# A gated recurrence and an MLP on one core: both MLP products regrouped from blocks of 256 and 192 columns to 38 products of blocks of 128

## The chip, the cores and the metric

The program runs on one core of a Trainium2 chip. TensorE (PE, with its weight loads as PEld) multiplies matrices into PSUM; VectorE (DVE), ScalarE (ACT) and GpSimd (POOL) work elementwise, POOL on SBUF alone; SyncE (SP) issues nearly all DMA transfers. Each engine takes its instructions in the order in which they were recorded and waits where data or a buffer is not ready. The metric is the device time of one execution in microseconds.

## The reference

A recurrence over 768 tokens, for 4 batches with 8 heads of 48 channels, and on its output a layer norm and an MLP with a residual:

```python
# q, k, v, alpha: (4, 8, 768, 48), float32
for t in range(S):
    state = alpha[:, :, t, :, None] * state + np.einsum('bhd,bhe->bhde', k[:, :, t], v[:, :, t])
    y[:, :, t] = np.einsum('bhd,bhde->bhe', q[:, :, t], state)
# x = y as (4, 768, 384)
mu = np.mean(x, axis=-1, keepdims=True)
var = np.mean((x - mu) ** 2, axis=-1, keepdims=True)
xn = (x - mu) / np.sqrt(var + 1e-06) * g_ln
ch = np.maximum(xn @ w_ch1, 0.0) @ w_ch2      # 384 -> 1536 -> 384, weights in float64
return (x + ch).astype(np.float32)
```

## The kernel before, in words

**Tiling.** The 768 tokens are 6 chunks of 128. Attention (`attention(c, b)`, L278) handles one chunk of one batch: 24 pieces of work, in which the recurrence becomes products of 64 or 128 tokens, and which ends with the normed tokens transposed into `xT` (3 blocks of 128 channels by 4 batches by 128 tokens). The MLP handles one chunk of all four batches at a time: `x` is 3 by 4 blocks of 128x128, `w1` 3 by 12, `w2` 12 by 3.

**The weights** arrive in float64 in 12 pieces of 768 KB through three staging buffers. `round_weights` (L207) makes float32 of a piece with five VectorE instructions of 768 columns and one of ScalarE.

**The MLP's products.** Chunk 0 uses the plain form: `hidden` (L499), 72 matmuls of 256 columns, and `project` (L514), 48 matmuls of 384 columns. Chunks 1 to 5 use schemes in the manner of Strassen, which trade products for sums of blocks: the first product is 15 products in place of 18 (`hidden_product`, L777; each 2 matmuls of 256 columns, done twice over), the second 20 in place of 24 (`product`, L611; each 4 matmuls of 192 columns). Sums of w1 (`combine_first`), of w2 (`combine_weights`), of x (`combine_x`) and of h (`combine_hidden`) are made on VectorE. Every product goes to a PSUM bank of its own; VectorE adds it to one or more results (L805 to L838, L628, L631), ScalarE copies some, and POOL makes late sums of intermediate results (L814 to L834, L634). ScalarE applies the relu (L846).

**The order of the work** is written out by hand in `ORDER` (L25), a string in which each letter lets one piece of work record its next few instructions, up to its next `yield` (L878): small letters are the 24 pieces of attention, A to L the weight pieces, Y and Z chunk 0's first product, P and Q its second, M the products of chunks 1 to 5, V the first product of the last chunk, S and W the weight sums, X and N the sums of x and h, R the relus, O the loads of the residual. Nothing reorders it: an instruction of an engine stands behind all that were recorded for this engine earlier.

**Buffers.** All PSUM tiles share 8 banks (tag `bank`). `hT` holds the hidden layer of a chunk; the last chunk's lies in buffers of attention that are free by then (`buffers_of_last`). Attention's results wait in DRAM (`kept`) and come back as the residual (`ob`).

Of the kernel before, what the change touches and what calls it, by code (L numbers as in the profile page):

```python
# [9 lines left out]
FP32 = mybir.dt.float32  # L10
# [13 lines left out]

ORDER = (  # L25
    "acacababcdaacabdbaabdcacabbacbbababceccbaAcfcdbadaacecacfeafdedebdfbeadbaedeecge"
    "adbAacgAfedghbgeedfecfafgfcefdAgeddbbgfdfghffbebaigcjbibffhjBhcdcYhCfcgccehYfedh"
    "cfedeedhgdedYjAfidBfjiBZhjhZZfBYegfhgjhghCiZYBYiCYYhfhghhkggZilihjZjgiZCiDjYDZZZ"
    "ghZYEYjkeiYkiDiEijgljjjlghYCYhiYkhYFEZhiFigYEZigkikDYZZlkkeejlYlgjhFlZlmYkZgknlg"
    "jZSGkHmiknlSljlkiljkjlGiHlmlllZimFhmZYgYmmjZiYhmheeHmGlkfSnZlnZefSQnmfiGHZghkkeo"  # L30
    "IYmSkiISkJgjIjommmOmJPJnSnQgopPghlKPIKhKjiPOnLSnSfSXkmQLffQOLXWkimXPQSWmPPXpnOpW"
    "XmnnXSmXSQomWnnpnmSoXmQMlmlkXkWliMnnMoXXpjWSWSMjMMoMoMlSMnMMWMoMknMMpMMqMMMMMOPi"
    "npnMopMMrmOMjkpMpopopRqoMoirQkplppnqprRppqWMMWMMnMWMqlMRrMMMMkMqRMMMjkrqRMrMMpsk"
    "oMoMMqMMRRnqpMMRjMqMMoWqOqsnRpqlsoqqpMsNtRNpMMNMjNoMoMMMosRqMMMOkNooMqtNMNMMMtMo"
    "MRlNNsmkNMpqMMNtMMMNlMrMMNMMNqMtqMsrMMWNnrrqMMMNMMstnMXvMsMMvXXprXorrXXXrqMMMXXM"
    "MMMMMMMsXqMMOmvMMMMMMMuXMMMMMMmtRMmttMRrtMrMMttrstvMtqussvsqtMMMMqMrMMrvMMMrRMMM"
    "MRMtMnMRMMmssmrMrrpOtsORMuRMoRMsMMMMoRNMMNtMMNMpqMMMoRNMRNMNNMMNRNOMnNMMMrstMpMN"
    "toNMNMMMMMrMnuoOMsMuNMvxMMuMNrpMOMNovMMvMMvMpMMMXtXMxvvMsXvssXXsXtvMXMuMXuXMMMMM"
    "usMMMtwMMMMMMvMMvwuuuRuuXuuuLxvXOMMMMMMMMMMMwMwxMrMuMswMuMMMwMMsvRxRvMMsMMRwMMxM"
    "xMqwMxMMxMwRtMMMxwMMMMxRqruwtxRwxswxxwRxwuxwRMNvNwMRMNrvwNRMMMMMMtNwNNquNNRrsvst"  # L40
    "tMNMJxMOMMMNNMxMMMvMqMuwxxMNtMtMMMMxuwXMwMMNXMXMMNMvNMXXuMXMXMMxXMXwMMXwMMMvMwMM"
    "MxMMMMMMMXMMMMMOuMuMMRMMMMMMMMwMMMMMMMMMRMMvxMMRMRxwMMMROMuMRMvOwxMMRRMwMRxMNMOM"
    "uMvMMXRVNMMMXXMMRMXXXXMMNVNVXVVXMVNMMVVVMVRVNXVVVVVNRVVMNXVVMVRVMVMVNVNMNVVVMVMV"
    "VMRVRVMVVVMVMVONVMVMNMVMMMRVMNNVRVVVVMVVROVMMMVMNVRVVRVMVMVMNMVRKMOMMMRNNMNMMNMM"
    "MMMNVNMNMNVMMMMNRONMMMNMMNMMMNMMMMNMMMNMMMMMMM"
# [4 lines left out]
def kernel(  # L50
# [41 lines left out]
    P = 128  # L92
# [89 lines left out]
    w1 = cpool.tile([P, NJ // 2, NF, 2 * P], FP32, name="w1")  # L182
# [9 lines left out]
    for i in range(NJ // 2):  # L192
        cs, js = slice(2 * i * P, 2 * (i + 1) * P), slice(2 * i, 2 * (i + 1))
        pieces.append((w1[:, i], w1_src[:, :, cs]))
        pieces.append((w2[:, js], w2_src[:, js]))
# [43 lines left out]
    more = cpool.tile([P, 4, NJ // 3 * DM // 2], FP32, name="more")  # L239
    zero = more.rearrange("p i m -> p (i m)")[:, 20 * P:21 * P]  # L240
    nc.vector.memset(zero, 0.0)
# [9 lines left out]
    eqs = [cpool.tile([P, NP, 2, 64], FP32, name=f"eq{b}") for b in range(2)]  # L251
    eqs += [shared[:, i * NP * P:(i + 1) * NP * P].rearrange(
        "p (a b c) -> p a b c", b=2, c=64) for i in range(2)]
    qks = [cpool.tile([P, 2, NP, 2, 64], FP32, name=f"qk{b}") for b in range(3)]
# [15 lines left out]
    ats = [cpool.tile([P, NP, 2, 2, HS], FP32, name=f"at{i}") for i in range(2)]  # L270
# [3 lines left out]
    x_of, xT_of, hT_of, las = ({} for _ in range(4))  # L274
# [3 lines left out]
    def attention(c, b):  # L278
# [52 lines left out]
        kT = work.tile([R, NP, 2, HS], FP32, name="kT", tag="sum", bufs=11)  # L331
        qT = work.tile([R, NP, 2, HS], FP32, name="qT", tag="sum", bufs=11)
# [60 lines left out]
        mid = None if whole else work.tile([R, NP, D], FP32, name="mid", tag="mid", bufs=3)  # L393
# [105 lines left out]
    def hidden(h, j):  # L499

        if 0 not in hT_of:
            hT_of[0] = work.tile([P, NJ, B, P], FP32, name="hT", tag="hT", bufs=1)
        bs = slice(2 * h, 2 * h + 2)
        hps = ps.tile([P, 2, P], FP32, name="hps", tag="bank", bufs=8)
        for f in range(NF):
            nc.tensor.matmul(hps, w1[:, j // 2, f, j % 2 * P:][:, :P], xT_of[0][:, f, bs],  # L506
                             start=(f == 0), stop=(f == NF - 1))
        yield
        nc.scalar.activation(out=hT_of[0][:, j, bs], in_=hps, func=AFT.Relu)
        yield  # L510

    ops_of, ob_of = {}, {}

    def project(c, b, js):  # L514
        if js[0] == 0:
            ops_of[b] = ps.tile([P, DM], FP32, name="ops", tag="bank", bufs=8)
        for j in js:
            nc.tensor.matmul(ops_of[b], hT_of[c][:, j, b], w2[:, j],  # L518
                             start=(j == 0), stop=(j == NJ - 1))
        yield  # L520
        if js[-1] == NJ - 1:
            nc.vector.tensor_add(ob_of[c, b], ops_of.pop(b), ob_of[c, b])
            send(c, b)
            yield

    HJ, HM, NT, HB = NJ // 2, DM // 2, NJ // 3, B // 2
    win, first_of, late_of = {}, {}, {}

    def third_of(c, t, h):

        if c + 1 == NCB:
            return late_of["h"][t * 2 + h]
        return hT_of[c][:, t * NT:(t + 1) * NT, h * HB:(h + 1) * HB]

    def buffers_of_last():

        more_x = work.tile([P, NF, B, P], FP32, name="xT", tag="xT").rearrange("p f b t -> p (f b t)")
        free = [raw.tile([P, 2, 2, NP, D], FP32, name=f"r{n}", tag="in", bufs=6).rearrange(  # L540
            "t b i p d -> t (b i p d)") for n in "akq"]
        h = [t.rearrange("k p i s t -> k (p i s t)") for t in ats]
        h += [t.rearrange("t n p i c -> t (n p i c)") for t in qks[:3]]
        h.append(more_x[:, :NT * HB * P])
        late_of["h"] = [t.rearrange("p (j b t) -> p j b t", b=HB, t=P) for t in h]
        sums = [t.rearrange("t p i c -> t (p i c)") for t in eqs[:2]]
        sums += [more_x[:, NT * HB * P:]] + [t[:, 512:] for t in free]
        late_of["x"] = [t[:, i * HB * P:(i + 1) * HB * P]
                        for t in sums for i in range(t.shape[1] // (HB * P))]
        late_of["u"] = [t[:, :512] for t in free]  # L550

    def weights_ready():

        if "b" not in win:
            b = {(t, h): w2[:, t * NT:(t + 1) * NT, h * HM:(h + 1) * HM]
                 for t in range(3) for h in range(2)}
            win["b"] = {4: b[2, 0], 7: b[0, 1], 11: b[2, 0], 14: b[1, 0], 15: b[1, 0], 17: b[0, 0]}
        return win["b"]

    def combine_weights():  # L560
        spare = [stage.tile([P, NF, 2 * P], INT64, name="ws", tag="ws") for _ in range(3)]
        spare = [t.rearrange("p a c -> p (a c)").bitcast(FP32) for t in spare]
        new = [t[:, i * NT * HM:][:, :NT * HM].rearrange("p (j m) -> p j m", m=HM)
               for t in spare for i in range(2)] + [
            more[:, i].rearrange("p (j m) -> p j m", m=HM) for i in range(4)]
        b = [w2[:, t * NT:(t + 1) * NT, h * HM:(h + 1) * HM] for t in range(3) for h in range(2)]
        t8, t9, t12, t1, n0, n6, n2, n13, n5, n10 = new
        add, sub = nc.vector.tensor_add, nc.vector.tensor_sub
        ready = weights_ready()
        for ns, op, o, x, y in (  # L570
                ((8,), add, t8, b[1], b[5]), ((12, 18), sub, t12, b[4], b[5]),
                ((1, 19), sub, t1, b[2], b[3]), ((9,), sub, t9, b[1], b[3]),
                ((6,), add, n6, t9, b[5]), ((), add, b[3], b[0], b[4]),
                ((3,), sub, b[5], b[3], b[2]), ((16,), sub, b[3], b[3], t8),
                ((2,), add, n2, t9, b[4]), ((5,), add, n5, t9, b[2]),
                ((10,), sub, n10, b[0], n5), ((0,), sub, n0, t8, b[2]),
                ((13,), sub, n13, t8, b[4])):
            op(o, x, y)
            ready |= {n: o for n in ns}
            yield  # L580

    def blocks_of(c):
        if c not in win:
            win[c] = a = [third_of(c, t, b // HB)[:, :, b % HB] for b in range(B) for t in range(3)]
            win["a", c] = {1: a[10], 3: a[0], 4: a[8], 10: a[3], 14: a[7], 16: a[9], 17: a[6],
                           18: a[5]}
        return win[c], win["a", c]

    def combine_hidden(c):
        a, ready = blocks_of(c)  # L590
        n0, n2, n6, n9, n5, n13 = (
            work.tile([P, NT, P], FP32, name=f"sum{i}", tag="sum", bufs=11) for i in range(6))
        add, sub = nc.vector.tensor_add, nc.vector.tensor_sub
# [315 lines left out]
```

## Time and profile before

| | us |
|---|---|
| median of 3 timed runs (lowest, highest) | 435.91 (434.07, 436.53) |
| span of the profiled execution, first to last instruction | 431.0 |
| PE busy, share of the span | 425.7 (99%) |
| weight loads (PEld) busy | 378.2 (88%) |
| VectorE busy | 333.2 (77%) |
| ScalarE busy | 200.0 (46%) |
| POOL busy | 152.7 (35%) |
| DMA moved | 45.53 MB |

The profile records one execution by itself; its own time is the span and what lies around it, which the page does not show. The median of the timed runs is 4.9 us longer than the span. Busy times are unions of the instructions' durations. A PE matmul's end is modelled, so starts are the safer measure for PE, and each float32 matmul leaves two records, each transpose one. Column counts are in the shapes: `128*128 128x256` is a load of 128x128 and a stream of 256 columns.

### The profile page before, as it was taken

How to read it: one execution, taken by the hardware profiler on the slowest of the kernel's cores; microseconds unless marked ns; L12 is line 12 of the kernel's file. 1: busy time of each engine (PE TensorE's matmuls, PEld its weight loads, DVE VectorE, ACT ScalarE, POOL GpSimd, SP SyncE). 2: the span in 40 equal slices, each digit the busy share in tenths (PEclk: the TensorE clock that was granted, in tenths of full speed). 3: DMA queues.
4: the chain of work that ended last, by engine and by line, in shares of the span. 5: the costliest groups of instructions: out<-in, count | busy, mean ns of one | idle time of the engine just before them, and what ended most of it. 6: DMA issues, size and time to landing. Idle time of an engine off the chain costs nothing.

```text
span 431.0 us, 11676 instructions
## 1 busy us (share of the span) xinstructions
PE 425.7 (99%) x4760; PEld 378.2 (88%) x4760; DVE 333.2 (77%) x644; ACT 200.0 (46%) x519; POOL 152.7 (35%) x164
## 2 busy tenths in 40 slices
PE   8999999999999999999999999999999999999997
PEld 6788888866588889998889998889998899999996
DVE  4989899999998888866769756757686668948683
ACT  6597466774043882325385134384415562221100
POOL 1011031110205382252563243580153661647423
PEclk9999999999999999999999999999999999999999
DMA  8979968774117354031150141400014000011201
GB/s 287 288 208 272 308 151 257 203 247 142 38 56 212 107 148 141 29 105 45 52 151 23 49 120 38 94 2 22 2 56 146 2 1 2 0 39 37 75 18 55
DMA packets 55517, 45.53 MB, mean 106 GB/s; under 512 B 26748, under 2 KB 51580, under 8 KB 55464
## 3 DMA queue, kind: packets, MB, share of 16 engines
q1 hardware_dynamic: 54920, 44.63, 35.0%
q8 instruction: 37, 0.61, 0.6%
q10 hardware_dynamic: 544, 0.17, 0.2%
q14 instruction: 16, 0.13, 0.1%
HBM read 35.25 MB, written 9.53 MB: 104 GB/s over the span
## 4 chain that ended last, share of the span: by engine, by line
PE 94%; DVE 2%; DMA 1%; ACT 1%; SPq 0%; issue 0%; DVEq 0%
PE hps L795 30%; PE ops L618 30%; PE ops L518 7%; PE hps L506 6%; PE tps L336 4%; PE aps L360 3%; PE ups L388 2%; PE yps L426 2%; PE yps L429 2%; PE xps L476 2%; DMA ws<-in_moe_w_ch_dram 1%; PE lps L303 1%; PE aps L352 1%; PE lps L244 1%; PE lps L298 1%; PE yps L414 1%
## 5 line engine op out<-in xcount | busy, mean ns | idle before, releaser
L795 PE MATMUL hps<-sum,w 128*128 128x256 f32 x192 | 48.0, 381 | 0.0
L634 POOL TENSOR_TENSOR ob<-ob,u 128x192 f32<-128x192 f32 x40 | 27.0, 685 | 58.9 <-DVE ob L631 44.3
L618 PE MATMUL ops<-w,hT 128*128 128x192 f32 x224 | 40.7, 328 | 0.0
L795 PEld LDWEIGHTS hps<-sum,w 128*128 128x128 f32 x192 | 35.7, 190 | 4.7 <-ACT hT L825 0.2
L618 PEld LDWEIGHTS ops<-w,hT 128*128 128x128 f32 x224 | 36.9, 190 | 1.0 <-issue 0.6
L403 POOL TENSOR_TENSOR mid<-mid,gate 112x192 f32<-112x192 f32 x20 | 13.3, 668 | 68.7 <-DVE mid L401 19.7
L795 PE MATMUL hps<-xT,w 128*128 128x256 f32 x136 | 34.4, 380 | 0.0
L506 PE MATMUL hps<-xT,w 128*128 128x256 f32 x144 | 34.0, 384 | 0.1
L846 ACT ACTIVATE hT<-hT 128x512 f32<-128x512 f32 x48 | 28.8, 625 | 10.4 <-POOL hT L817 7.1
L518 PE MATMUL ops<-w,hT 128*128 128x384 f32 x96 | 32.8, 490 | 0.0
L628 DVE TENSOR_TENSOR ob<-ops,ob 128x192 f32<-128x192 f32 x50 | 17.6, 353 | 17.7 <-PE ops L618 9.4
L506 PEld LDWEIGHTS hps<-xT,w 128*128 128x128 f32 x144 | 26.3, 190 | 4.0 <-DVE xT L479 0.6
L618 PE MATMUL ops<-ws,sum 128*128 128x192 f32 x160 | 29.2, 327 | 0.0
L814 POOL TENSOR_TENSOR hT<-hT,u 128x512 f32<-128x512 f32 x8 | 10.4, 1305 | 53.0 <-DVE u L813 53.0
L795 PEld LDWEIGHTS hps<-xT,w 128*128 128x128 f32 x136 | 25.5, 190 | 3.2
L518 PEld LDWEIGHTS ops<-w,hT 128*128 128x128 f32 x96 | 17.6, 190 | 10.5
L618 PEld LDWEIGHTS ops<-ws,sum 128*128 128x128 f32 x160 | 26.4, 190 | 0.2
L336 PE MATMUL tps<-consts,qk 128*112 128x128 f32 x176 | 25.3, 275 | 0.2 <-DVE qk L311 0.2
L336 PEld LDWEIGHTS tps<-consts,qk 128*112 128x112 f32 x176 | 20.3, 134 | 4.3 <-DVE qk L311 0.8
L460 ACT ACTIVATE xn<-x,few 128x384 f32<-128x384 f32 x24 | 14.8, 615 | 18.7 <-DVE few L456 17.5
L618 PE MATMUL ops<-ws,hT 128*128 128x192 f32 x128 | 23.4, 327 | 0.0
L618 PE MATMUL ops<-more,sum 128*128 128x192 f32 x120 | 22.0, 327 | 0.0
(243 smaller groups left out, 1172.9 us busy)
## 6 DMA issues: line engine op xcount, KB each, us to landing
ws<-in_moe_w_ch_dram SPq DMA_DIRECT2D x12, 768.0 KB
vn<-in_v_dram SPq DMA_DIRECT2D x12, 384.0 KB
kept<-x SPq DMA_DIRECT2D x24, 192.0 KB
ob<-kept SPq DMA_DIRECT2D x24, 192.0 KB
out_dram<-ob SPq DMA_DIRECT2D x19, 192.0 KB
ra<-in_alpha_dram SPq DMA_DIRECT2D x14, 192.0 KB
rk<-in_k_dram SPq DMA_DIRECT2D x6, 384.0 KB
rq<-in_q_dram SPq DMA_DIRECT2D x6, 384.0 KB
```

What stands on the lines that cost most here:

```text
L336: nc.tensor.transpose(tps[:, p], qk_of(c, b)[:, i, p].rearrange("p a b -> p (a b)")[:, :R], ident)
L360: nc.tensor.matmul(aps[0][halves[i if cross else 1 - i], p, s], kT[rs, p, s], qT[rs, p, s], start=True, stop=True)
L403: nc.gpsimd.tensor_mul(new, new, by)
L460: act(out=xn, in_=x, func=AFT.Square, bias=mean, accum_out=dev)
L506: nc.tensor.matmul(hps, w1[:, j // 2, f, j % 2 * P:][:, :P], xT_of[0][:, f, bs], start=(f == 0), stop=(f == NF - 1))
L518: nc.tensor.matmul(ops_of[b], hT_of[c][:, j, b], w2[:, j], start=(j == 0), stop=(j == NJ - 1))
L618: nc.tensor.matmul(acc, lhs[:, j], rhs[:, j], start=(j == 0), stop=(j == NT - 1))
L628: nc.vector.tensor_add(x, acc, x)
L634: getattr(nc.gpsimd, f"tensor_{op}")(x, x, y)
L795: nc.tensor.matmul(acc[:, i], w, b, start=True, stop=True)
L814: add_late(c4, c4, u2)
L846: nc.scalar.activation(out=x, in_=x, func=AFT.Relu)
```

## The change

Both products of the MLP become one scheme of 38 products for what is plainly 48 products of blocks. A block of the weights is now a quarter of the 12 column blocks (3 of 128), and a block of tokens is one batch (128 tokens), so that each of the 38 products is 3 matmuls that load 128x128 and stream 128 columns. This holds for the first product of chunks 1 to 5 and the second of chunks 0 to 5, so chunk 0's plain second product goes. Chunk 0's first product stays as it was.

- Products are gathered in chains in PSUM (`start` and `stop` in the tables): a bank is read by VectorE or ScalarE while its chain goes on, and later products add onto what it already holds. POOL's late sums of results go.
- Sums of x (32 a chunk, 128 columns), of h (36 a chunk, 384 columns), of w1 and of w2 (32, 384 columns) are made on VectorE or POOL, as the tables `WHERE` say one by one; also whether a result's first copy and its relu are VectorE's or ScalarE's.
- 18 sums of w1 don't fit in SBUF: they are written to DRAM once (`keep`) and read again in each of the chunks 1 to 5 into a ring of four buffers (`weights_again`).
- `hT` and the last chunk's hidden layer (`late`) have buffers of their own; attention's `at`, `qk` and `eq` now lie in `late`. The buffers for sums go from 11 to 9, those of `mid` from 3 to 2.
- `ORDER` is written anew.

```diff
+SUMS = 9
+MORE, RING, STREAMED = 8, 4, 18
+FIRST_TEMPS, SECOND_TEMPS = 6, 6
...
+FIRST_PRODUCTS = (
+    (0, 2, 6, 1, 0, ((14, -1),)), (30, 12, 7, 1, 0, ((11, 1),)),
+    (18, 14, 5, 1, 0, ((8, 1), (9, 1))), (1, 6, 4, 1, 0, ((2, 1), (10, -1))),
...
+SECOND_PRODUCTS = (
+    (26, 17, 6, 1, 0, ((2, -1),)), (27, 16, 5, 1, 0, ((2, -1),)),
+    (5, 18, 7, 1, 0, ((7, 1), (10, -1))), (29, 3, 5, 0, 0, ((0, 1),)), (12, 7, 6, 0, 0, ()),
...
-    w1 = cpool.tile([P, NJ // 2, NF, 2 * P], FP32, name="w1")
+    w1 = cpool.tile([P, NF, NJ * P], FP32, name="w1")
...
+    hT = cpool.tile([P, NJ, B, P], FP32, name="hT")
+    late = cpool.tile([P, NJ * B * P], FP32, name="late")
...
-    ats = [cpool.tile([P, NP, 2, 2, HS], FP32, name=f"at{i}") for i in range(2)]
+    ats = [late[:, 2 * i * NP * P:2 * (i + 1) * NP * P].rearrange(
+        "p (a i s t) -> p a i s t", i=2, s=2, t=HS) for i in range(2)]
...
-        for j in js:
-            nc.tensor.matmul(ops_of[b], hT_of[c][:, j, b], w2[:, j],
-                             start=(j == 0), stop=(j == NJ - 1))
...
+    def sum_up(turn, kind, out, x, y):
+        e = nc.gpsimd if kind != "n" and other(turn) else nc.vector
...
+    def sums_of_first_weights():
+        for step in FIRST_WEIGHTS:
+            if step[0] == "keep":
+                _, n, i = step
+                kept_w[n] = dram.tile([P, G, P], FP32, name="wk", tag="wk", bufs=STREAMED)
+                nc.sync.dma_start(kept_w[n], first_weight(i))
+            else:
+                to, x, y, kind = step
+                sum_up("S", kind, first_weight(to), first_weight(x), first_weight(y))
+            yield
...
+    def weights_again():
+        for c in range(1, NCB):
+            for w, *_ in FIRST_PRODUCTS:
+                if w >= len(FIRST_HOMES):
+                    ring[c, w] = work.tile([P, G, P], FP32, name="wr", tag="wr", bufs=RING)
+                    nc.sync.dma_start(ring[c, w], kept_w[w])
+                    yield
...
+    def first_products(c):
+        for w, x, chain, start, stop, reads in FIRST_PRODUCTS:
+            if start:
+                accs["f", c, chain] = ps.tile([P, G, P], FP32, name="hps", tag="bank", bufs=8)
+            acc, lhs, rhs = accs["f", c, chain], first_weight(w, c), x_at(c, x)
+            for j in range(G):
+                nc.tensor.matmul(acc[:, j], lhs[:, j], rhs, start=bool(start and j == 0), stop=bool(stop),
+                                 skip_group_check=True)
+            yield
+            for o, sign in reads:
+                out = h_of(c)[:, o // B * G:(o // B + 1) * G, o % B]
+                if ("f", c, o) not in done:
+                    done.add(("f", c, o))
+                    if other("M" if c + 1 < NCB else "V"):
+                        nc.vector.tensor_scalar(out=out, in0=acc, scalar1=float(sign), scalar2=None,
+                                                op0=AOP.mult)
+                    elif sign > 0:
+                        nc.scalar.copy(out=out, in_=acc)
+                    else:
+                        nc.scalar.mul(out, acc, -1.0)
+                elif sign > 0:
+                    nc.vector.tensor_add(out, acc, out)
+                else:
+                    nc.vector.tensor_sub(out, out, acc)
+            yield
...
+    def second_products(c):
+        left = {b: sum(o // NF == b for *_, reads in SECOND_PRODUCTS for o, _ in reads) for b in range(B)}
+        for w, h, chain, start, stop, reads in SECOND_PRODUCTS:
+            if start:
+                accs["s", c, chain] = ps.tile([P, P], FP32, name="ops", tag="bank", bufs=8)
+            acc, lhs, rhs = accs["s", c, chain], h_at(c, h), second_weight(w)
+            for j in range(G):
+                nc.tensor.matmul(acc, lhs[:, j], rhs[:, j], start=bool(start and j == 0),
+                                 stop=bool(stop and j == G - 1), skip_group_check=True)
+            yield
+            for o, sign in reads:
+                b, m = divmod(o, NF)
+                out = ob_of[c, b][:, m * P:(m + 1) * P]
+                (nc.vector.tensor_add if sign > 0 else nc.vector.tensor_sub)(out, out, acc)
+                left[b] -= 1
+                if not left[b]:
+                    send(c, b)
+            yield
...
     def mlp():
-        for c in range(1, NCB):
-            if c + 1 < NCB:
-                yield from hidden_products(c)
-            for n in SECOND:
-                yield from product(c, n)
+        for c in range(NCB):
+            if c and c + 1 < NCB:
+                yield from first_products(c)
+            yield from second_products(c)
```

In the tables, a product's row is: number of the weight sum, number of the x or h sum, chain, whether it starts or stops the chain, and the results that read the bank after it, with their signs. Lines L743 and L780 of the changed kernel are the matmuls of the first and the second products, L754 to L760 and L786 their reads, L697 to L701 the sums, L708 and L724 the transfers of the kept sums, L768 and L770 the relus.

## The prediction

> **What bounds the kernel now.** I read the page's busy shares first, then busy time by stretch, the chain, the shapes, and single instructions for start-to-start times.
>
> ```profile
> span 431.0 us, 11676 instructions
> ## 1 busy us (share of the span) xinstructions
> PE 425.7 (99%) x4760; PEld 378.2 (88%) x4760; DVE 333.2 (77%) x644; ACT 200.0 (46%) x519; POOL 152.7 (35%) x164
> ...
> PE 94%; DVE 2%; DMA 1%; ACT 1%; SPq 0%; issue 0%; DVEq 0%
> ```
>
> The chain is 94% PE: TensorE is the bound, and what shortens its stream shortens the kernel, as long as it is fed. The stretches show how close the others are:
>
> ```profile
> core 0: us, PE busy (x) PEld busy (x) DVE busy (x) ACT busy (x) POOL busy (x), PEclk, DMA share, GB/s
> 0.00:20.00 20.00, 17.94 (x182) 14.17 (x183) 12.65 (x31) 11.51 (x25) 2.04 (x6) 1.00 0.94 291
> 30.00:70.00 40.00, 39.86 (x725) 34.01 (x717) 35.64 (x62) 24.57 (x65) 6.11 (x9) 1.00 0.85 255
> 70.00:120.00 50.00, 50.00 (x584) 35.52 (x584) 47.15 (x82) 26.66 (x69) 5.92 (x9) 1.00 0.56 163
> 170.00:431.00 261.00, 257.89 (x2255) 242.06 (x2253) 185.31 (x376) 99.07 (x260) 114.56 (x118) 1.00 0.17 50
> ```
>
> Up to 120 us VectorE is 89 to 94% busy beside a full PE: a second bound, nearly reached. After 170 us it is 71% busy, and the DMA engines are nearly free. From PE's real pitch, its work reached 26.3 us with 21.0 us done, and 425.5 us with 420.1 done: PE runs 5.3 us behind its own sum, lost in the start, and nothing later. So the span is the sum of PE's pitches (422.4) + 5.3 + 3.3 after the last matmul.
>
> The pitches: the chain gives 18.21/112 = 163 ns a record at 192 columns (two records to an fp32 matmul); likewise 216 at 256 and 322.5 at 384: 0.83 ns a column and some 3 ns.
>
> ```profile
> 409.69 18.21 PE ops L618 x112
> ```
> ```profile
> 16.18 1.16 PE L352 MATMUL aps<-qT,kT 48*128 48x128 f32 x16
> ```
>
> No row has a warm product of 128x128 with 128 columns. The transposes L476 start 109 ns apart, but load faster. L352 is nearest: 128 columns loaded, 128 streamed, two row halves in turn; in the trace each half starts every 111.5 ns once it runs.
>
> **The change, part by part.**
>
> *TensorE.* Out: 300 matmuls of 256 columns (129.5 us), 400 of 192 (130.0) and chunk 0's 48 of 384 (31.0): 290.5 us. In: 11 sets of 38 x 3 = 1254 matmuls of 128 columns, 2508 records. At L476's 109.2 ns 273.9 us, at L352's 111.5 ns 279.6. Bounds of the gain: 16.6 and 10.9; I take 10.9, since L352's loads are as long as its streams. Attention and chunk 0's first product keep their count and shapes, only their places move.
>
> The Trainium skill (TensorE: Matmul & The Clock Gate, "Back-to-back issue gap") says that in a stream of load and matmul pairs both set the spacing, about 81 ns at 128 columns where the isolated gap is 56. Were those 25 ns added here, it would be an estimated 63 us more and this change a heavy loss; L352's 111.5 beside 109.2 does not bear that out, though it fills half the rows.
>
> *VectorE.* An add from PSUM takes 353 ns at 192 columns (L628), 553 at 384 (L522) and 692 at 512 (L807), about 1.05 ns a column; of each, 83 ns lie under the next instruction. Pitches: 203 ns at 128, 470 at 384, 603 at 512.
>
> ```profile
> L628 DVE TENSOR_TENSOR ob<-ops,ob 128x192 f32<-128x192 f32 x50 | 17.6, 353 | 17.7 <-PE ops L618 9.4 <-ACT u L678 3.2 <-ACT u L665 2.4
> L634 POOL TENSOR_TENSOR ob<-ob,u 128x192 f32<-128x192 f32 x40 | 27.0, 685 | 58.9 <-DVE ob L631 44.3
> L814 POOL TENSOR_TENSOR hT<-hT,u 128x512 f32<-128x512 f32 x8 | 10.4, 1305 | 53.0 <-DVE u L813 53.0
> ```
>
> Reads of the second products: 124 instructions (34.2 us) become 276 of 128 columns (56.1); of the first: 120 (72.3) become 214 of 384 (100.4); sums of x, h and weights 167 (88.4) become 184 (69.7), since POOL takes 253 more of them; 22 relus move in (5.9). Sum 308.6 to 345.8 us.
>
> *POOL.* Its undisturbed ops take 590 ns at 192 and 1272 at 512 columns, so 454 at 128 and 1000 at 384. Late adds of 113 us go, 253 sums of 188 come: 135.9 to 210.5 us. ACT stays (189 to 187).
>
> *DMA and SP.* 18 sums of w1 are written (3.5 MB) and read 5 times (17.7 MB, 90 issues): 44.8 to 66.0 MB. In a chunk's first product the reloads make 3.5 MB in 25 us, 141 GB/s, on top of 129 at 120 to 170 us: under the 291 that the first 20 us show, so I cost them nothing. SP's 103 more issues stand behind output and gate transfers that wait; a blocked one delays a reload, and with a ring of four buffers PE has some 5 us (four times 25/18) before it would notice.
>
> *The new order.* Each engine takes its instructions in the written order; against the trace of before, neighbours in that order on PE and VectorE start within 4 us of each other. So I summed each engine's work between the same points of PE's own work:
>
> | PE's work, us | VectorE before | after | POOL before | after |
> |---|---|---|---|---|
> | 20 to 61 | 36.9 | 46.3 | 6.5 | 6.6 |
> | 61 to 112 | 45.7 | 52.7 | 4.1 | 50.1 |
> | 112 to 162 | 41.9 | 41.1 | 20.8 | 23.6 |
> | 162 to 400 | 152.0 | 183.5 | 96.8 | 127.2 |
>
> Chunk 0's second product now needs all of w2 rounded, its 32 weight sums and 36 sums of h first, so the rounding (47 us, 60 instructions) ends by point 81, where before 13.1 us of it lay beyond 84.
>
> First stretch: 46.3 us beside 41.4 of PE. VectorE at 100% costs PE 4.9 us, at the 94% of 70 to 120 us 7.9; I take 6: rounding has hardly any waits but its transfers. By point 60, 20.5 MB are asked for (17.3 before); 20.5/0.291 = 70 us is earlier than VectorE's 74, so DMA is not the later one.
>
> Second stretch: VectorE 52.7 beside PE's 50.6 and POOL's 50.1. And these two hinder each other:
>
> ```profile
> 388.53 0.69 DVE L605 TENSOR_TENSOR sum<-hT,sum 128x512 f32<-128x512 f32 x1
> 389.13 1.76 DVE L605 TENSOR_TENSOR sum<-sum,hT 128x512 f32<-128x512 f32 x1
> ```
> ```profile
> 388.69 1.65 POOL L814 TENSOR_TENSOR qk<-qk,rq 128x512 f32<-128x512 f32 x1 [1.49 <-DVE rq L813]
> ```
>
> The same add takes 0.69 us, then 1.76 under a POOL sum, which itself takes 1.65 for 1.27. Over all such overlaps POOL loses 0.58 us for each us of VectorE work with two SBUF inputs. That work is 30.5 us here: POOL 50.1 + 17.7 = 67.8 us. Bounds: 52.7 (+2.1) and 67.8 (+17.2). I take +9: POOL's sums of w1 aren't due until point 122 and may trail, those of w2 and h may not, and VectorE at 94% alone gives +5.4.
>
> Third stretch: PE is longest, 0. Later, POOL exceeds PE at points 152 to 172, 223 to 243 and 274 to 294 once the 0.58 is added (23.8, 21.0, 22.2 against 20.3): 0 to 6, taken 2.
>
> Sum: -10.9 + 6 + 9 + 2 = +6.1: span 437. What lies outside the span is 435.9 - 431.0 = 4.9 us, the median of the runs over the profile; it stays. **442 us**, 1.4% slower. Ends: -16.6 + 4.9 + 2.1 = -9.6 (426), -10.9 + 7.9 + 17.2 + 6 = +20 (456).
>
> **The rivals.**
>
> 1. *The early work has slack.* PE's stream holds more attention ahead (22.4 us in the second stretch, 13.0 before), which needs none of the late sums. Then VectorE's and POOL's load is made up after point 112, where they have 9 and 26 us spare in 50. Loss only 0 to 5: 435.9 - 16.6 + 0 to 5 = 419 to 424. Against it: VectorE already trails by up to 3 us there, and the order puts no PE work ahead of it. It decides if PE loses under 8 us before chunk 1's first product.
> 2. *The loads set the pace.* Each product loads 128 columns per 128 streamed. A short run of L352 takes 1.16 us for 8 records of a half: 145 ns; 2508 of them 364 us, +73: 509. Against: the cold matmuls L244 (both 128x128) start 213 ns apart, twice L476's 109, with loads as long as the streams: no sign of a wait for the load. The page named above would put it near there.
> 3. *Reads in between hold the chains.* A product waits until VectorE has read its bank. In a first product VectorE has 20.1 us of reads and 1.2 of relus in 25 of PE, 14.5 before. Were 2 us lost in each of 5 chunks, beside the forecast's 6: about 452.
> 4. *Reloads land late*: 18 x 5 at 0.1 us each, +9: about 451.
>
> **Chances.** Forecast 0.5, rival 1 0.28, rival 2 0.04, rival 3 0.12, rival 4 0.06. Half a per cent, 2.2 us, is what a measurement here can tell. The forecast's cases fall 0.09 within that bound, 0.41 slower; rival 1 0.26 faster, 0.02 within. Faster 0.26, same 0.11, slower 0.63. Range 421 to 458: it cuts the best of rival 1 and all of rival 2; the forecast's own is 434 to 450.
>
> **What would show it.** L780 and L743 at 109 to 112 ns a record; PE's idle 15 to 25 us, nearly all before 130 us, ended by VectorE and POOL; VectorE over 95% busy from 25 to 125 us; POOL's sums of 384 columns well over 1.0 us there; after 140 us PE full. I am wrong if PE is full before 130 us, if the records are over 115 ns, or if idle time is spread over the chunks.

## The result: 495 us, slower than before, and the profile after

The changed kernel takes 495.25 us (median of 4 runs, 493.6 to 498.6) where the kernel before takes 434.99 on the same chip: a ratio of 1.139, 95% interval 1.134 to 1.145. The forecast was 442, with a range of 421 to 458. Its sign was right, its size was far off: some 60 us slower, where 6 were forecast.

The page of the changed kernel, its first lines and the first line of its chain:

```profile
span 494.5 us, 14491 instructions
## 1 busy us (share of the span) xinstructions
PE 448.2 (91%) x5772; PEld 414.2 (84%) x5772; DVE 424.3 (86%) x929; ACT 197.8 (40%) x518; POOL 243.5 (49%) x297
...
PE 50%; DVE 32%; issue 6%; DMA 4%; ACT 4%; POOL 2%; SPq 1%; DVEq 0%; POOLq 0%; ACTq 0%
```

The chain was 94% PE, now half of it is something else, and the largest part of that is VectorE. Busy time by stretch, first two stretches of the kernel before (its first 20 us stand in the prediction), then five of the changed kernel:

```profile
20.00:82.00 62.00, 61.86 (x1190) 53.85 (x1189) 55.76 (x99) 44.06 (x117) 10.42 (x15) 1.00 0.82 240
82.00:160.00 78.00, 78.00 (x997) 59.18 (x995) 70.56 (x125) 41.02 (x106) 21.25 (x21) 1.00 0.47 139
```
```profile
core 0: us, PE busy (x) PEld busy (x) DVE busy (x) ACT busy (x) POOL busy (x), PEclk, DMA share, GB/s
0.00:20.00 20.00, 16.63 (x116) 11.90 (x117) 9.65 (x25) 9.09 (x19) 2.04 (x6) 1.00 0.83 260
20.00:82.00 62.00, 56.80 (x1005) 47.27 (x1004) 58.73 (x95) 37.43 (x94) 9.30 (x12) 0.97 0.81 235
82.00:160.00 78.00, 58.19 (x900) 50.16 (x893) 77.35 (x126) 33.66 (x95) 55.41 (x53) 0.93 0.44 128
160.00:300.00 140.00, 135.76 (x1950) 129.46 (x1949) 119.70 (x287) 63.98 (x170) 78.50 (x104) 1.00 0.51 150
300.00:500.00 200.00, 180.78 (x1826) 175.40 (x1825) 158.86 (x400) 53.65 (x144) 98.29 (x124) 0.99 0.27 81
```

From 82 to 160 us PE was full before and is now busy for 58 of 78 us, while VectorE is 99% busy beside a POOL that is 71% busy. The clock granted to TensorE was 0.93 in that stretch, 1.00 before; over 78 us that is at most some 5 us of PE's time, a part that no run here separates. The chain in those stretches shows what VectorE does there, and one run of the new products at their own pace:

```profile
128.34 3.52 DVE hT L697
...
142.63 2.09 DVE hT L697
...
151.09 3.44 DVE sum L697
...
376.77 10.06 PE hps L743 x90
```

The last line is 111.8 ns a record: the products cost what the sum assumed. The first three are single sums of 384 columns, an instruction that takes 0.55 us undisturbed.

As in the prediction I put PE's time against its own work: the sum of its records' pitches, a pitch being the time from one start to the next when nothing holds PE (new records at the measured 111.7 ns). What it takes beyond that is its loss. All its work is 412.0 us, where the forecast had 422.4 - 10.9 = 411.5. So the span 494.5 = 412.0 + 79.2 lost + 3.3 behind the last matmul. By stretches of PE's work:

| PE's loss, us, in its work | to 21 | 21 to 63 | 63 to 112 | 112 to 162 | 162 to 399 |
|---|---|---|---|---|---|
| before | 5.3 | 0.7 | -0.9 | -0.7 | 0.9 |
| after | 12.1 | 9.5 | 29.0 | 3.7 | 24.8 |
| forecast of the difference | 0 | 6 | 9 | 0 | 2 |
| measured difference | 6.8 | 8.8 | 29.9 | 4.4 | 23.9 |

Two terms carry most of the miss: the second stretch (63 to 112), 21 us too small, and the time after 162 us, 22 too small. The start and the first stretch (to 63) add 10, the third (112 to 162) 4.

### The profile page after: what moved, and what is told of

Read it like the earlier page. It is cut to its first block, busy times and chain, and to the rows that moved or that the text cites. A ratio compares the mean times of both kernels' runs of the same rounds, so it can differ in the third digit from the quotient of the medians.

```text
span 494.5 us, 14491 instructions
## 1 busy us (share of the span) xinstructions
PE 448.2 (91%) x5772; PEld 414.2 (84%) x5772; DVE 424.3 (86%) x929; ACT 197.8 (40%) x518; POOL 243.5 (49%) x297
## 4 chain that ended last, share of the span: by engine, by line
PE 50%; DVE 32%; issue 6%; DMA 4%; ACT 4%; POOL 2%; SPq 1%; DVEq 0%; POOLq 0%; ACTq 0%
PE hps L743 19%; PE ops L780 18%; DVE ob L786 4%; DVE hT L697 2%; PE tps L463 2%; DVE sum L699 2%; DMA ra<-in_alpha_dram 2%; PE aps L487 2%; PE lps L430 2%; DVE sum L701 2%; DVE sum L697 1%; PE yps L556 1%; DMA vx<-in_v_dram 1%; DVE hT L768 1%; DVE ws L347 1%
## 5 line engine op out<-in xcount | busy, mean ns | idle before, releaser
L786 DVE TENSOR_TENSOR ob<-ob,ops 128x128 f32<-128x128 f32 x276 | 68.5, 279 | 25.3 <-PE ops L780 24.1
L780 PE MATMUL ops<-w,sum 128*128 128x128 f32 x396 | 54.4, 279 | 6.2 <-DVE ob L786 3.0
L780 PEld LDWEIGHTS ops<-w,sum 128*128 128x128 f32 x396 | 48.5, 192 | 8.9 <-DVE sum L697 3.3
L758 DVE TENSOR_TENSOR hT<-hps,hT 128x384 f32<-128x384 f32 x76 | 40.1, 549 | 5.5 <-PE hps L743 2.2
L760 DVE TENSOR_TENSOR hT<-hT,hps 128x384 f32<-128x384 f32 x72 | 38.1, 547 | 4.6 <-ACT hT L754 1.5
L743 PE MATMUL hps<-xT,w 128*128 128x128 f32 x300 | 39.5, 275 | 0.0
L743 PE MATMUL hps<-xs,wr 128*128 128x128 f32 x270 | 37.5, 278 | 0.9 <-ACT late L754 0.6
L743 PEld LDWEIGHTS hps<-xT,w 128*128 128x128 f32 x300 | 36.4, 192 | 0.1
L743 PE MATMUL hps<-xT,wr 128*128 128x128 f32 x270 | 35.9, 276 | 0.6 <-ACT few L586 0.5
L631 PE MATMUL hps<-xT,w 128*128 128x256 f32 x144 | 34.2, 385 | 0.9 <-DVE mid L528 0.9
L743 PEld LDWEIGHTS hps<-xs,wr 128*128 128x128 f32 x270 | 33.3, 192 | 1.7 <-ACT late L754 0.8
L743 PEld LDWEIGHTS hps<-xT,wr 128*128 128x128 f32 x270 | 32.8, 192 | 1.6 <-ACT few L586 0.7
L780 PE MATMUL ops<-ws,hT 128*128 128x128 f32 x210 | 29.5, 279 | 1.9 <-DVE ob L786 1.4
L780 PE MATMUL ops<-ws,sum 128*128 128x128 f32 x180 | 26.1, 283 | 5.5 <-DVE ws L699 2.9
L780 PE MATMUL ops<-more,hT 128*128 128x128 f32 x210 | 28.9, 277 | 1.6 <-DVE ob L786 1.6
L780 PEld LDWEIGHTS ops<-ws,hT 128*128 128x128 f32 x210 | 26.0, 192 | 3.4 <-DVE ob L786 2.3
L780 PEld LDWEIGHTS ops<-ws,sum 128*128 128x128 f32 x180 | 22.4, 192 | 7.1 <-DVE ws L699 3.1
```

The lines of the kernel that those rows point to most:

```text
L631: nc.tensor.matmul(hps, w1[:, f, j * P:(j + 1) * P], xT_of[0][:, f, bs], start=(f == 0), stop=(f == NF - 1))
L743: nc.tensor.matmul(acc[:, j], lhs[:, j], rhs, start=bool(start and j == 0), stop=bool(stop), skip_group_check=True)
L758: nc.vector.tensor_add(out, acc, out)
L760: nc.vector.tensor_sub(out, out, acc)
L780: nc.tensor.matmul(acc, lhs[:, j], rhs[:, j], start=bool(start and j == 0), stop=bool(stop and j == G - 1), skip_group_check=True)
L786: (nc.vector.tensor_add if sign > 0 else nc.vector.tensor_sub)(out, out, acc)
```

## Experiments

For every run that keeps PE's matmuls, PE's loss is its span less 412.0 + 3.3. In e12 PE's work is 417.5: 48 matmuls of 384 columns (31.0 us) for 114 of 128 (25.5).

| kernel | median us | ratio to before (95%) | span | PE's loss |
|---|---|---|---|---|
| changed kernel | 495.25 | 1.134 to 1.145 | 494.5 | 79.2 |
| POOL's sums as memsets (e2) | 451.89 | 1.035 to 1.047 | 450.2 | 34.9 |
| no reloads (e3) | 494.34 | 1.134 to 1.142 | 492.3 | 77.0 |
| fresh bank after a read (e4) | 490.69 | 1.125 to 1.136 | 487.9 | 72.6 |
| late sums all on POOL (e6) | 520.89 | 1.191 to 1.205 | 521.1 | 105.8 |
| early sums all on VectorE (e7) | 491.47 | 1.129 to 1.138 | 489.9 | 74.6 |
| start in the old order (e8) | 498.07 | 1.144 to 1.154 | 496.6 | 81.3 |
| VectorE's sums as memsets (e9) | 459.02 | 1.050 to 1.060 | 458.4 | 43.1 |
| fewer, wider sums on VectorE (e10) | 495.91 | 1.137 to 1.147 | 492.9 | 77.6 |
| copies and relus on ScalarE (e11) | 490.64 | 1.123 to 1.133 | 489.8 | 74.5 |
| plain second product of chunk 0 (e12) | 499.23 | 1.139 to 1.153 | 497.4 | 76.6 |
| all sums on VectorE (e13) | 513.56 | 1.175 to 1.185 | 511.7 | 96.4 |
| the same, copies on ScalarE (e14) | 502.52 | 1.151 to 1.160 | 500.2 | 84.9 |
| the same, all sums of x on POOL (e15) | 494.06 | 1.129 to 1.140 | 493.2 | 77.9 |

### Is it the meeting of VectorE and POOL, and is it the chains or the reloads?

The instruction rows by themselves (e1):

> This kernel leaves the whole computation out: it runs rows of 12 or 24 equal VectorE instructions alone, and the same rows beside back-to-back GpSimd sums, copies or memsets on other buffers, with nothing to wait for in between. Theory A (VectorE's instructions with two SBUF inputs starve while GpSimd reads SBUF): the 384-column add takes some 470 ns from start to start alone and 770 or more beside GpSimd's 384-column adds (0.64 ns more for each ns of overlap), with single ones far longer; the same add beside memsets stays near 470; an add that reads PSUM, and one-input instructions, lose less than half as much. Rival B (the long instructions in the changed kernel were waits for data that the profile counts as busy): the add takes 470 to 500 ns in every row.

Here the rows were laid out by a scheduler that mixed them, so the table wanted did not come out. Rows of VectorE's and POOL's 384-column adds did run beside each other, both at 1267 ns from start to start, and among 24 one-input instructions one took 6.0 us. Rival B fell, and Theory A got a sharper form, tested in e5.

POOL's sums without reading (e2):

```diff
+        if e is nc.gpsimd:
+            e.memset(out, 0.0)
-        if kind == "n":
+        elif kind == "n":
```

> GpSimd's 253 sums are replaced by memsets of the same blocks, so they read nothing and wait for no input: their results, and with them the output, are left out. VectorE keeps every instruction. Theory A (GpSimd's reading hinders VectorE, and GpSimd's own lengthened sums come late): VectorE's instructions go back to their undisturbed lengths, its sum of durations from 482 us to some 430, and the time falls by 30 us or more, to 440 to 465. Rival C (VectorE has too many instructions in too short a stretch, whoever is beside it): under 15 us, 480 or more. Rivals D (reloads late) and E (reads hold the chains): under 10 us.

451.9 us. VectorE does the same 929 instructions and is busy for 370.6 us where it was 424.3. Theory A, inside its bracket.

```profile
PE 432.5 (96%) x5772; PEld 407.8 (91%) x5772; DVE 370.6 (82%) x929; ACT 197.7 (44%) x518; POOL 104.8 (23%) x297
```

VectorE's 35 sums of 384 columns that start between 82 and 160 us take 1.11 us in the mean in the changed kernel, the longest 4.86; beside the memsets 43 such sums take 0.56, the longest 0.86. But the memsets also spare POOL work and waits (104.8 us busy for 243.5), so not all of the 43 us need be the meeting; the mirror of this run, e9, keeps POOL's sums.

Without reloads (e3):

```diff
-                    ring[c, w] = work.tile([P, G, P], FP32, name="wr", tag="wr", bufs=RING)
-                    nc.sync.dma_start(ring[c, w], kept_w[w])
+                    ring[c, w] = first_weight(w % len(FIRST_HOMES))
```

> The 90 reloads of w1's sums are left out (the products that would use them multiply by one of the 16 resident blocks, so the output is left out), with 17.7 MB of DMA and 90 issues on SP. Theory A: within 1% of the changed kernel, 490 to 498. Rival D (reloads land late, or their traffic holds the residual, gate and output transfers): 10 us or more faster, PE's idle time after 160 us halved.

494.3: the intervals of the two kernels lie over each other. The reloads cost nothing that can be measured.

A fresh bank after each read (e4):

```diff
+            start = start or (c, chain) in read
+            read.discard((c, chain))
+            if reads and not stop:
+                read.add((c, chain))
             if start:
                 accs["f", c, chain] = ps.tile([P, G, P], FP32, name="hps", tag="bank", bufs=8)
```

(and the same lines in the second products)

> A product that follows a read of its chain opens a new PSUM bank with a new start instead of adding onto the bank that is being read, so no product waits for a read of its own chain; what the chain held before is lost to the later reads, so the output is left out. Instructions and their order stay. Theory A: VectorE's order is unchanged and is what is late, so within 1.5% of the changed kernel, 488 to 503. Rival E (reads in between hold the chains): 12 us or more faster, and the stalls of PE after 160 us go from some 24 us to under 12.

490.7, some 5 us less than the changed kernel, with intervals that just overlap. Rival E's 12 us are not there; PE's loss after 162 us goes from 24.8 to 19.6. Reads in between cost at most a few us, the mechanism of rival 3 at about half its price.

### What a meeting costs

> The computation is left out again: 12 equal VectorE instructions alone, 12 equal GpSimd ones alone, then both kinds beside each other, each pair on a line of its own and with nothing to wait for. The mixed rows of the first such kernel let me state Theory A sharper: an instruction of VectorE that reads two SBUF inputs and one of GpSimd that reads SBUF go one for one, so the 384-column adds of both start every 1267 ns together (469 and 950 alone), a 128-column add of VectorE beside 384-column sums of GpSimd starts every 1000 to 1150 ns instead of 203, and beside memsets nothing changes. Instructions that read PSUM stay at 465 and 203 ns. For VectorE's one-input relu from SBUF the theory has no number: 300 to 530 ns alone, and single ones of several us beside GpSimd, as the first kernel had one of 6.0 us. Rival G (the two share a bandwidth, and each slows in proportion to the other's columns): the 128-column add beside 384-column sums starts every 300 to 450 ns.

The groups of this kernel, twelve VectorE instructions in each row; the lines with POOL are its rows beside them. L39 is the add alone, L73 POOL's 384-column add alone, L90 and L91 the two beside each other; L96 is the 128-column add beside L97, L102 the add from PSUM and L120 the relu beside 384-column sums, L150 the add beside memsets:

```profile
L39 DVE TENSOR_TENSOR dv<-da,db 128x384 f32<-128x384 f32 x12 | 5.7, 550 | 0.0
L73 POOL TENSOR_TENSOR pv<-pa,pb 128x384 f32<-128x384 f32 x12 | 11.4, 986 | 0.0
L90 DVE TENSOR_TENSOR dv<-da,db 128x384 f32<-128x384 f32 x12 | 14.5, 1278 | 0.0
L91 POOL TENSOR_TENSOR pv<-pa,pb 128x384 f32<-128x384 f32 x16 | 19.1, 1231 | 0.0
L96 DVE TENSOR_TENSOR dv<-da,db 128x128 f32<-128x128 f32 x12 | 12.1, 1083 | 0.0
L97 POOL TENSOR_TENSOR pv<-pa,pb 128x384 f32<-128x384 f32 x16 | 15.8, 1024 | 0.0
L102 DVE TENSOR_TENSOR dv<-acc,da 128x384 f32<-128x384 f32 x12 | 5.7, 542 | 0.0
L120 DVE TENSOR_SCALAR dv<-da 128x384 f32<-128x384 f32 x12 | 11.3, 1011 | 0.0
L150 DVE TENSOR_TENSOR dv<-da,db 128x384 f32<-128x384 f32 x12 | 5.7, 553 | 0.0
L105 DVE TENSOR_TENSOR tv<-tv,tp 128x4 f32<-128x4 f32 x1 | 15.2, 15164 | 8.9 <-POOL tp L104 8.9
```

From start to start, in ns, for rows that had settled:

| VectorE's instruction | alone | beside POOL's 384-column adds (949 alone) |
|---|---|---|
| add of two SBUF blocks, 384 columns | 469 | 1267 |
| add of two SBUF blocks, 128 columns | 202 | 1000 |
| relu from SBUF, 384 columns | 269 | 1067 |
| add from PSUM, 384 columns | 465 | 465 |
| add of two SBUF blocks beside memsets | 469 | 469 |

In these rows every meeting that holds VectorE adds 798 ns, whatever its instruction: the pair takes both their times less 151 ns (469 + 949 - 151 = 1267, 202 + 949 - 151 = 1000, 269 + 949 - 151 = 1067; with a 128-column POOL sum 469 + 410 - 151 = 728, measured 726). They go one after the other. What reads PSUM is not touched, nor is the add beside memsets, which read nothing. Rival G's 300 to 450 ns for the narrow add is out.

The Trainium skill (SBUF — State Buffer, "Who interferes with whom") says that VectorE's second read interface is GpSimd's only one, and that the pair is an exclusive lock: an instruction with two SBUF inputs and one of GpSimd that reads SBUF block each other fully, where a write alone does not. The rows agree in all of this. The prediction did not use that page.

And VectorE can lose its turn for longer than one instruction: the 4-column add L105 took 15.16 us, the whole row of sixteen POOL sums at its side. That is what the chain's 3.52 us is. VectorE and POOL in the changed kernel, from 127.7 us:

```profile
128.15 0.27 DVE L786 TENSOR_TENSOR ob<-ob,ops 128x128 f32<-128x128 f32 x1
128.34 3.52 DVE L697 TENSOR_TENSOR hT<-sum,hT 128x384 f32<-128x384 f32 x1
131.79 0.55 DVE L697 TENSOR_TENSOR ra<-w 128x384 f32<-128x384 f32 x1
...
127.83 0.76 POOL L530 TENSOR_TENSOR st<-st,gate 112x192 f32<-112x192 f32 x1 [2.97 <-DVE st L528]
128.55 0.99 POOL L697 TENSOR_TENSOR ws<-w,ws 128x384 f32<-128x384 f32 x1
129.51 0.99 POOL L701 TENSOR_TENSOR ws<-ws,more 128x384 f32<-128x384 f32 x1
130.46 0.99 POOL L697 TENSOR_TENSOR ra<-w,ws 128x384 f32<-128x384 f32 x1
```

A sum of h that chunk 0's second product needs stands from 128.3 to 131.9 us behind POOL's attention instruction and three sums of weights in a row, which themselves run at their undisturbed 0.99 us. The profile counts all of it as VectorE being busy.

### Moving the sums

Late sums on POOL (e6): `WHERE["X"]` all "1", `WHERE["N"]` all "1" behind chunk 0's 36.

> All sums of x, and of h from chunk 1 on, go to GpSimd: 78 sums of 384 columns and 56 of 128 leave VectorE (47.9 us of its pitches) and add 100 us to GpSimd's 244. Theory A: VectorE has then nearly no instruction with two SBUF inputs after 160 us, so the loss of PE there falls by what the meetings of the two cost and not by what GpSimd's longer row costs: PE's loss after 160 us of its work from 29 to 10 to 20 us, 476 to 488. Rival F (it is GpSimd's sums that come late, whoever is beside them): GpSimd becomes the later one, 505 or more.

520.9, rival F. VectorE has 134 sums fewer and is busy for 371.7 us, POOL for 326.4, and now PE waits for POOL itself; the first and second of PE's waits after 180 us (us in total, times, longest):

```profile
PE ops L775 <- POOL sum L694: 12.3, 10, 1.7
PE ops L775 <- POOL hT L694: 5.5, 4, 2.0
```

Early sums on VectorE (e7): `WHERE["S"]`, `WHERE["W"]` and the first 36 of `WHERE["N"]` all "0".

> All sums of w1 and w2, and chunk 0's sums of h, go to VectorE: 35 and 17 instructions of 384 columns, 24.4 us more for VectorE, 49 us less for GpSimd, which is then idle from 60 to 112 us of PE's work. Theory A (meeting GpSimd costs VectorE there some 20 us): the 24 us more and the 20 us less nearly cancel, 490 to 502. Rival C (VectorE's count alone): 495 + 24, 515 to 520.

491.5: VectorE took 24.4 us more, yet its busy time fell a little (420.0 us), and PE's loss in the second stretch went from 29.0 to some 23. As Theory A had it, POOL's help there was worth nothing.

The start in the old order (e8): the first 280 letters of the old `ORDER`, then the new one without those.

> The first 280 letters of the order are those of the kernel before (attention, the first weight pieces and chunk 0's first product), the rest is the changed kernel's order without what has then been done; all instructions are the same. It asks what the 16 us that PE loses beyond the kernel before in its first 63 us of work come from. Theory H (the new order of the start: transfers and the gate columns behind others on SP's queue): most of the 16 us go, and about 10 of them stay gained to the end, 482 to 488. Rival I (VectorE has to do the rounding for the second stretch anyway, so a better start is lost again by 105 us of PE's work): 491 to 497.

498.1, so rival I, and a little beyond its bracket. PE's loss to 21 us of its work is 5.1 as before the change, and at 63 us it is 21.5, as in the changed kernel (21.6). The stretches of this kernel to 82 us:

```profile
0.00:20.00 20.00, 17.44 (x188) 14.01 (x189) 12.62 (x32) 11.67 (x25) 2.04 (x6) 1.00 0.96 287
20.00:82.00 62.00, 49.64 (x943) 42.21 (x942) 55.77 (x88) 37.92 (x97) 8.68 (x13) 0.93 0.78 225
```

VectorE is busy for 68.4 us of the first 82 in all three kernels (12.65 + 55.76 before, 9.65 + 58.73 after, 12.62 + 55.77 here), but the new order asks for 67.9 us of its work by PE's point 63, where the old one asks for 56.9. A better start of PE made no difference here to when VectorE is through.

VectorE's sums without reading (e9): the edit of e2 with `nc.vector` in place of `nc.gpsimd`.

> The mirror of the run with GpSimd's memsets: now VectorE's 158 sums and 5 copies with a sign become memsets of the same blocks (the output is left out), and GpSimd keeps all its 253 sums with their waits. VectorE keeps its reads of PSUM, the rounding and the relus. Theory A (it is VectorE, held at each instruction with two SBUF inputs, that makes PE wait): nearly as good as the other one, 452 to 470. Rival F (GpSimd's sums come late by themselves, as they did when they got all the late sums): 478 or more.

459.0, inside Theory A's bracket. (VectorE's memsets are 184 by the trace: 177 sums and 7 with a sign, not the 158 and 5 of the expectation.) Whichever side stops reading, most of the loss after 82 us goes. Here VectorE is spared its own sums' work too, as POOL was in e2; what both runs share is that the sums of the two no longer meet. From 82 to 160 us, first with POOL's memsets (e2), then with VectorE's (e9):

```profile
82.00:160.00 78.00, 73.31 (x1206) 66.78 (x1199) 69.13 (x168) 43.72 (x118) 28.70 (x67) 0.96 0.63 184
```
```profile
82.00:160.00 78.00, 69.67 (x1159) 63.65 (x1159) 62.83 (x157) 38.52 (x105) 59.99 (x64) 0.93 0.58 167
```

PE has 73.3 and 69.7 us of work in where it had 58.2; POOL, in e9, has all its sums and 60.0 us.

Fewer, wider sums on VectorE (e10): `WHERE["X"]` all "1" behind chunk 1's, 18 of the later ones in `WHERE["N"]`, evenly spread, from "1" to "0".

> From the sums of chunk 2's x on, 41 sums of x (128 columns) go from VectorE to GpSimd and 18 sums of h (384 columns) from GpSimd to VectorE: the undisturbed work of both engines stays (VectorE 8.3 us out, 8.4 in; GpSimd 16.8 in, 17.1 out), but VectorE has 23 instructions with two SBUF inputs fewer. Theory A (one for one, so that an instruction costs VectorE the same 0.8 us whatever its width): up to 18 us less of VectorE's time, of which PE gets about half: 483 to 490. Rival G (the loss goes by columns): 493 to 497.

495.9: no gain. VectorE's busy time fell, 424.3 to 419.3, where Theory A allowed up to 18 us, and PE did not wait less. The time lies in rival G's bracket, which the 128-column rows of e5 speak against. I take it that it counts which sum is late, not how many there are; no run shows that.

Copies and relus on ScalarE (e11): `WHERE["M"]`, `WHERE["V"]` and `WHERE["R"]` all "0".

> VectorE's 29 first reads and 22 relus go to ScalarE, which is 40% busy. VectorE loses 13.5 us of PSUM reads that no GpSimd sum delays and 5.9 us of relus that cost 269 ns alone and 1067 beside GpSimd. Theory A: VectorE is what PE waits for after 160 us, so 5 to 14 us faster than the changed kernel, 481 to 490. Rival J (a read by ScalarE comes later than one by VectorE, and holds the chain longer): 494 or more.

490.6: some 5 us, just outside the bracket, for 22.8 us less of VectorE's busy time (401.5).

Chunk 0's second product plain (e12): `plain_second()` with 48 matmuls of 384 columns and 4 adds, no sums of h for chunk 0, the letters W moved behind chunk 0's last M, one after every second M of chunk 1.

> Chunk 0's second product is plain again, 48 matmuls of 384 columns: PE has 5.6 us more, chunk 0's 36 sums of h and its 46 narrow reads go (4 wide reads come), and the 32 sums of w2 move into chunk 1's first product. Theory A (the sums and GpSimd beside the rounding are what PE waits for between 63 and 105 us of its work): the loss there falls from 29 to about 10 us, 3 to 5 of it come back in chunk 1's first product: 476 to 486. Rival C' (VectorE's rounding and reads alone fill it): 490 or more.

499.2: the total lies in the bracket of rival C', yet the second stretch went as Theory A had it. From 63 to 112 us of PE's work the loss falls from 29.0 to 9.9, as expected; from 112 to 162 it rises from 3.7 to 17.6, where 3 to 5 were expected. The 32 sums of w2 stand there now, and I take it that they are what costs this time; the run does not separate them.

All sums on VectorE (e13): `WHERE["S"]`, `["W"]`, `["N"]`, `["X"]` all "0".

> All 253 sums of GpSimd go to VectorE (154 of 384 columns, 99 of 128: 92.2 us of its pitches); GpSimd keeps only attention's 44 us. Theory A (an instruction of VectorE and one of GpSimd that meet go one after the other, so that GpSimd's sums save VectorE little): VectorE's busy time is the 371 us that it had beside the memsets plus 92, so 463, plus some 10 to 25 us of its idle time at the start and the end: 473 to 492, no slower than the changed kernel although VectorE has 158 + 253 sums. Rival C (VectorE's count of work as it stands, 424 busy, plus 92): 560 or more. Rival F is not touched by it.

513.6. Both numbers missed, from both sides. The page:

```profile
PE 454.7 (89%) x5772; PEld 416.7 (81%) x5772; DVE 454.0 (89%) x1182; ACT 198.6 (39%) x518; POOL 31.3 (6%) x44
```

VectorE is busy for 454.0 us against 424.3. So the 253 sums for which POOL was busy 212 us more (243.5 - 31.3) saved VectorE 30 us, not the 92 of their pitches there, and the kernel 18. But with 89% on PE and on VectorE neither is full: each waits for the other in turn, in an order that counts on two engines for the sums, and I take the 22 us above the bracket to be that. How much another order would win back was not tried.

The same with copies on ScalarE (e14), and then with all 155 sums of x on POOL, where the changed kernel has 99 (e15):

> As the run before, and the 29 first reads and 22 relus go to ScalarE (13.5 + 5.9 us off VectorE). Theory A: VectorE busy 444, so 455 to 475 in all, clearly faster than the changed kernel. Rival C: 540 or more.

> As the run before, but the 155 sums of x (128 columns) are GpSimd's: 31.3 us off VectorE, 64 us for GpSimd. By the pairs measured alone a 384-column sum of VectorE that meets a 128-column one of GpSimd takes 726 ns for 469, and a 128-column one 460 for 203: 0.26 us a meeting, at most 40 us for all 155. Theory A: between 9 us slower and 31 us faster than the run before, likeliest 5 to 15 faster, 450 to 465.

502.5 and 494.1. The differences come out (11 us less for 19.6 us off VectorE; 8.5 less for the sums of x, in the 5 to 15), the levels lie some 30 us above their brackets, I take it for the reason given for e13. No version that computes the whole thing came below 490 us, and without POOL's reading it is still 452: nothing here beats the kernel before.

## Why the prediction was wrong, step by step

- **TensorE, -10.9:** right. Records start 111.7 ns apart (taken: 111.5), PE's work is 412.0 for 411.5. Rival 2 is out: nothing of the 145 ns of a short run, nor of the estimate from the Trainium skill's page (TensorE: Matmul & The Clock Gate, "Back-to-back issue gap"), shows in these records.
- **First stretch and the start, +6:** measured 6.8 + 8.8 = 15.6. The bound named, VectorE with the rounding, is right, but the term was made for the work from 20 to 61 alone and took VectorE as level with PE at 20. VectorE's idle time from the start (7.4 us in the first 20 us, 10.4 in the changed kernel) belongs to the sum: work asked for by a point, plus the idle time up to then. With the 67.9 us asked for by point 63 and the 13.6 us that it is idle in the first 82 in all three kernels, that is 81.5 of the 84.6 us after which PE gets there; e8 shows that a better start of PE does not change it. A smaller part the prediction did not have at all: L339, the first step of rounding, against L217:

```profile
L339 DVE TENSOR_SCALAR w<-ws x12: 546/942/1366, 25.4 to 94.8; 128x768 int32<-128x768 int32 x12
```
```profile
L217 DVE TENSOR_SCALAR w<-ws x12: 545/552/561, 21.4 to 103.3; 128x768 int32<-128x768 int32 x12
```

  The six pieces of w1 take 0.94 us where they took 0.55, those of w2 do not: 2.3 us. w1's new layout writes each piece as three strips of 256 columns, before it was one strip of 768. That this is the cause is argued, not tried; the Trainium skill (VectorE: DVE Perf Modes, "Mode 2×_2P — use both read ports for one tensor") asks for an even outermost dimension, or an odd one that is equal on both sides, and the output's is now 3.
- **Second stretch, +9:** measured 29.9. This is the step that failed. It said "POOL loses 0.58 us for each us of VectorE work with two SBUF inputs" and charged POOL alone: 67.8 us at worst, VectorE left at its undisturbed 52.7. The row shown beside it (0.69 us, then 1.76) was VectorE's loss, and it was quoted and not priced. By the pairs of e5 the two go one after the other. Then the stretch has 30.5 us of VectorE's two-input work plus 50.1 of POOL's, 80.6, less 0.15 for each of some 50 meetings: 73 to 81 us beside PE's 50.6, +22 to +30, if the rest of VectorE's work fits beside POOL's. The prediction held both numbers; they had to be added, not compared. That this sum reaches the 29.9 is partly luck: by the same measure PE still loses some 11 us of this stretch in e2 and some 16 in e9, where the sums of the two no longer meet. So the meetings are worth some 13 to 18 us of the 29.0 lost there. The rest stays open: VectorE comes into the stretch late and has more work in it than PE, and the granted clock is lower.
- **After 162 us, +2:** measured 23.9, the same step: here too the 0.58 was put on POOL alone. Without the meetings PE loses 5.0 there (e2) or 8.0 (e9). "After 140 us PE full" fell with it, and so did its sign of being wrong, "idle time spread over the chunks", which is what came.
- **Third stretch, 0:** 4.4, trailing sums. **Reloads at nothing:** right (e3); rival 4 is out. **Rival 3:** its reads hold PE for at most some 5 us in all (e4). **Rival 1**, slack in the early work, allowed PE a loss of under 8 us before chunk 1's first product; by point 112 it had lost 50.6.
- **What lies around the span, 4.9:** the changed kernel's profiled execution took 496.3 us for its span of 494.5, so 1.8. The 4.9 was a median less one execution's span.

Put right, the sum is -10.4 + 15.6 + 29.9 + 4.4 + 23.9 = +63.4 on a span of 431.0.

## What to carry to other kernels

Before work is split between VectorE and POOL, sort VectorE's instructions: those that read PSUM lay beside POOL's sums unharmed, those with two SBUF inputs did not, nor did the one-input relu from SBUF, and in a stretch where both are dense their times add up. A busy VectorE is no proof of work: compare a group's mean and its longest instruction with the undisturbed ones (1.11 and 4.86 us for 0.56 and 0.86 here), as an instruction that stands and waits for POOL looks busy. And a second bound that is 94% full takes its idle time at the start with it: sum its work to a due point, and its idle time, from the beginning of the program, not from the stretch.

## What was not expected of the hardware

A meeting costs VectorE 0.8 us beside a 384-column POOL sum whether its own instruction has 384, 128 or 4 columns (the 4-column add of e5 takes some 0.16 us alone, and 0.93 in four places where a row of POOL's 384-column sums has just begun); a waiting instruction can be passed over for a whole row of POOL's (15.16 us beside sixteen sums, 3.52 us beside three in the kernel), though in other rows the two take turns one for one. And a one-input relu from SBUF, 269 ns alone, is held too: 1067 ns beside POOL's sums, 567 even beside its memsets.
